# The output stores of an attention and FFN kernel, issued from ScalarE's queue in place of SyncE's

## The chip, the cores and the metric

The kernel runs on one core of one Trainium2 chip. The metric is the device time of one execution in microseconds. Three executions of the kernel before took 586.12, 587.52 and 589.68 us; the median is 587.52.

The engines are named as the profile names them: PE is the matrix engine (PEld its weight loads), DVE the vector engine, ACT the scalar engine, POOL GpSimd, and SP the sync engine, which does no arithmetic here and issues DMAs. A name with a q (SPq, ACTq) is the queue of that engine, where DMAs are issued and semaphores waited for.

## The reference

The function is a "talking heads" attention followed by a feed-forward network with a squared ReLU. Batch is 8, heads 12, sequence 448, head dimension 64, model dimension 768, hidden dimension 2048.

```python
scores = scale * np.matmul(q, k.transpose(0, 1, 3, 2))
scores = np.einsum('bhij,hg->bgij', scores, w_pre)      # heads mixed before the softmax
scores = scores - np.max(scores, axis=-1, keepdims=True)
attn = np.exp(scores)
attn = attn / (np.sum(attn, axis=-1, keepdims=True) + 1e-09)
attn = np.einsum('bhij,hg->bgij', attn, w_post)         # and after it
x = np.matmul(attn, v)                                  # transposed to (3584, 768)
h = np.maximum(x @ w_in, 0.0)
out = h * h @ w_out                                     # (3584, 768), float32
```

## The kernel before, in words

One program holds everything. The attention of a batch is cut into 45 steps of 10 query rows (`NT` = 45, `IQ` = 10). With 12 heads a step has 120 rows, one for each pair of query and head, so that the mixing of heads is a matmul over 120 partitions. There are 360 steps in all. The main loop over `i` makes, in each step, these pieces:

- `mix` (L415): one matmul (L426) mixes the heads of the gathered scores `G` into a PSUM bank `m_ps`; ACT takes the exponential with its row sum (L430) into `e`. Every second step DVE makes the reciprocals (L437) and POOL scales the second mixing matrix with them, `pn` (L440).
- `unmix` (L446), `LAG` = 4 steps later: matmuls of `e` with `pn` (L455, L459) into `at_ps`, which DVE copies (L461).
- `gather` (L382), up to `AHEAD` = 10 steps ahead: DMAs from SP's queue (L394, L397) that bring the scores of 10 queries of all heads from the score tile `S` into a `G` tile. `S` has two buffers, and `G` twelve.
- `score_burst` (L353): the matmuls of queries and keys (L365, L371) for six heads at once, each into a PSUM bank of its own; ACT (L375) and DVE (L377) copy them to `S`, about half each. A batch after the first takes seven bursts.
- `av_unit` (L221): after each third of a batch, the product with the values, copied by ACT to `xt` (L242).

Between these, `fill` lets out pieces of the feed-forward network of the batch before, which wait in a list with a cost each. `ffn1_unit` is the first matrix (L283), ReLU on ACT (L289) and a square on POOL (L295). `ffn2_unit` (L322) is the second matrix: 16 matmuls of 384 columns (L328) in two parts into one PSUM bank `o_ps`, and then a copy by DVE to half of an `osb` tile of 128 rows (L337). After the second half of a tile, `store_rows` (L305) stores its 128 rows. It issues one DMA for each stretch of up to `PQ` = 64 rows, because the rows of the output are interleaved over the sequence; so a tile of 128 rows needs two DMAs of 192 KB each, or one DMA for either of two batches where the tile holds the last 64 rows of both. That makes 54 DMAs in 27 pairs. `osb` has two buffers. The very last tile is stored in another way, by `last_store` (L313), half from SP's queue and half from ACT's.

All PSUM banks come from one pool of eight (`psp`, L77). The order of the instructions on PE and POOL is the order of the program text (`manual_schedule(engines={PE, POOL})`, L483). The order on ACT, DVE and SP, and with it the place of each store in its queue, is set by the framework's scheduler when the program is built. Each DMA from SP or ACT signals its landing on one of eight semaphores in turn, and before a DMA is issued its queue waits for the landing of the one that used the same semaphore before it.

Of the kernel before, what the change touches and what calls it, by code (L numbers as in the profile page):

```python
# [55 lines left out]
def kernel(  # L56
# [11 lines left out]
    nc = tc.nc  # L68
# [33 lines left out]
    def wcol(w, name, eng):  # L102
# [7 lines left out]
                      in_=bass.AP(tensor=w_pre.tensor, offset=w_pre[0, 0:1].offset, ap=[[0, P], [1, H * H]]))  # L110
# [24 lines left out]
    for t in range(3 * P // IQ, NT):  # L135
        n0, n = max(0, 3 * P - IQ * t), min(IQ, S - IQ * t)
# [166 lines left out]
    out_rows = out.rearrange("(b p r) m -> b r p m", b=B, r=RQ)  # L303

    def store_rows(b, t, end, osb, j):  # L305
        while t < end:
            r, p = divmod(t, PQ)
            n = min(end - t, PQ - p)
            nc.sync.dma_start(out=out_rows[b, r, p:p + n, :], in_=osb[j:j + n, :])
            t += n  # L310
            j += n

# [9 lines left out]
    def ffn2_unit(b, mt, nt, part):  # L322
        if part == 0:
            o_open[(b, mt, nt)] = bank("o_ps")
        ps = o_open[(b, mt, nt)]
        for ft in range(8 * part, 8 * part + 8):
            lhsT = h2ts[(b, ft // 2)][:, ft % 2, mt * P:mt * P + P] if mt < 3 else tails[:, ft, :]
            nc.tensor.matmul(ps[:, 0:384], lhsT=lhsT, rhs=w2[ft // 4][:, ft % 4, nt * 384:(nt + 1) * 384],  # L328
                             start=(ft == 0), stop=(ft == FT - 1))
        if part == 0:  # L330
            return
        if nt == 0:
            osbs[b] = ffnp.tile([P, DMODEL], F32, name="osb", tag="osb", bufs=2)
        if b == B - 1 and mt == 3:
            last_store(b, nt, osbs[b], ps)
            return
        nc.vector.tensor_copy(out=osbs[b][:, 384 * nt:384 * nt + 384], in_=ps[:, 0:384])  # L337
        if nt == 1 and mt < 3:
            store_rows(b, P * mt, P * mt + P, osbs[b], 0)
        elif nt == 1:  # L340
            store_rows(b - 1, MAIN, S, osbs[b], 0)
            store_rows(b, MAIN, S, osbs[b], 64)
# [140 lines left out]
    with tc.manual_schedule(engines={PE, POOL}):  # L483
# [40 lines left out]
        for i in range(-1, end):  # L524
# [9 lines left out]
            if s0:  # L534
                b, t = s0
# [75 lines left out]
```

## Time and profile before

| | before |
|---|---|
| median of three executions | 587.52 us |
| profiled execution, its own time | 588.54 us |
| its span, first to last instruction | 586.8 us |
| granted PE clock, mean | 0.996 |
| busy: PE, DVE, ACT, POOL | 563.8, 399.0, 379.6, 353.7 us |
| `store_rows`, issues on SP's queue | 54, of 466 to 1548 ns each, median 744 |
| first and last of them | 114.0 and 578.2 us |
| `gather`, issues of L394 on SP's queue | 312, of 672 to 2103 ns each, median 774 |
| DMAs issued on ACT's queue | 6: two at the start, four in `last_store` |

The busy times are those of one profiled execution. They overlap, so they don't add up to the span. Issuing a DMA or waiting for a semaphore doesn't count as busy time of ACT or SP: such time is found in the timeline of their queues. In lines of groups and waits, "out<-in" are tile names with buffer numbers left out. A line of waits gives who waited, for whom, the total in us, how often, and the longest; a line of the timeline gives the start in us, the length in us, the engine, the line and the operation, and in square brackets the idle time just before it and what ended that. The chain of work that ended last is followed back from the last instruction, and its rows give a start, a length and what ran.

### The profile page before, as it was taken

How to read it: one execution, taken by the hardware profiler on the slowest of the kernel's cores; microseconds unless marked ns; L12 is line 12 of the kernel's file. 1: busy time of each engine (PE TensorE's matmuls, PEld its weight loads, DVE VectorE, ACT ScalarE, POOL GpSimd, SP SyncE). 2: the span in 40 equal slices, each digit the busy share in tenths (PEclk: the TensorE clock that was granted, in tenths of full speed). 3: DMA queues.
4: the chain of work that ended last, by engine and by line, in shares of the span. 5: the costliest groups of instructions: out<-in, count | busy, mean ns of one | idle time of the engine just before them, and what ended most of it. 6: DMA issues, size and time to landing. Idle time of an engine off the chain costs nothing.

```text
span 586.8 us, 18426 instructions
## 1 busy us (share of the span) xinstructions
PE 563.8 (96%) x6735; PEld 363.8 (62%) x6735; DVE 399.0 (68%) x979; ACT 379.6 (65%) x1090; POOL 353.7 (60%) x796
## 2 busy tenths in 40 slices
PE   4999978999999999999999999999999999999996
PEld 2577767756566566566665665666565666666554
DVE  7748947868777677866977678767877668655011
ACT  3747967678876557875776558775777548862410
POOL 6566983574777338773678437783487436772730
PEclk9999998999999999999999999999999999999999
DMA  9999998596578864796559954788544865432113
GB/s 130 150 194 176 190 202 174 106 186 154 119 127 142 158 123 88 125 153 145 103 101 139 169 110 97 119 140 158 107 72 71 138 131 107 82 50 55 28 27 82
DMA packets 85579, 72.28 MB, mean 123 GB/s; under 512 B 18768, under 2 KB 80496, under 8 KB 85488
## 3 DMA queue, kind: packets, MB, share of 16 engines
q1 hardware_dynamic: 49354, 47.30, 36.5%
q0 software_dynamic: 35552, 23.60, 30.9%
q8 instruction: 53, 0.87, 0.6%
q10 hardware_dynamic: 582, 0.21, 0.2%
q14 instruction: 38, 0.31, 0.1%
HBM read 47.28 MB, written 11.01 MB: 99 GB/s over the span
## 4 chain that ended last, share of the span: by engine, by line
PE 91%; DMA 3%; ACT 3%; POOL 1%; DVE 1%; issue 1%; ACTq 0%; POOLq 0%
PE o_ps L328 25%; PE h_ps L283 25%; PE m_ps L426 11%; PE at_ps L455 10%; PE ot_ps L229 5%; PE s_ps L365 5%; PE m_ps L412 4%; DMA G<-S 2%; PE tr_ps L214 2%; PE ot_ps L236 2%; PE at_ps L459 2%; ACT e L430 1%; PE s_ps L371 1%; ACT S L375 1%; DMA kst<-in_k_dram 1%
## 5 line engine op out<-in xcount | busy, mean ns | idle before, releaser
L430 ACT ACTIVATE e<-m_ps 120x448 bf16<-120x448 f32 x360 | 196.1, 551 | 86.8 <-PE m_ps L426 46.7
L461 DVE CAST at<-at_ps 128x480 bf16<-128x480 f32 (+1 forms) x360 | 206.6, 593 | 65.9 <-PE at_ps L459 49.0
L440 POOL TENSOR_SCALAR pn<-post,rc 120x120 bf16<-120x120 bf16 (+1 forms) x340 | 123.4, 373 | 170.8 <-DVE rc L437 106.1
L283 PE MATMUL h_ps<-xt,w 128*128 128x448 bf16 (+2 forms) x960 | 167.2, 317 | 0.2
L328 PE MATMUL o_ps<-w,h 128*128 128x384 bf16 x768 | 138.7, 326 | 0.1
L426 PE MATMUL m_ps<-G,pre 120*120 120x448 bf16 (+1 forms) x340 | 121.8, 359 | 4.6 <-ACT S L375 3.1
L455 PE MATMUL at_ps<-pn,e 120*128 120x120 bf16 x1080 | 116.0, 216 | 4.3 <-ACT S L375 2.8
L283 PEld LDWEIGHTS <-w 128*128 128x128 bf16 x960 | 84.6, 99 | 53.4 <-issue 4.3
L455 PEld LDWEIGHTS <-e 120*128 120x128 bf16 x1080 | 86.0, 98 | 49.5 <-ACT S L375 5.4
L295 POOL TENSOR_TENSOR h<-hr 128x384 bf16<-128x384 f32 (+1 forms) x128 | 103.2, 807 | 20.4 <-ACT hr L289 19.1
L328 PEld LDWEIGHTS <-h 128*128 128x128 bf16 x768 | 72.9, 98 | 47.9 <-issue 4.9
L289 ACT ACTIVATE hr<-h_ps 128x448 f32<-128x448 f32 (+2 forms) x136 | 71.8, 530 | 45.4 <-PE h_ps L283 36.0
L375 ACT CAST S<-s_ps 128x448 bf16<-128x448 f32 x177 | 82.2, 550 | 15.3 <-PE s_ps L365 9.5
L377 DVE CAST S<-s_ps 128x448 bf16<-128x448 f32 x141 | 79.9, 615 | 5.1 <-DMA G<-S 4.3
L430 ACT ACTIVATION_READ_ACCUMULATOR e<-m_ps 120x1 f32 x360 | 75.5, 210 | 0.0
L337 DVE COPY osb<-o_ps 128x384 f32<-128x384 f32 x54 | 30.1, 557 | 57.6 <-PE o_ps L328 57.4
L437 DVE RECIPROCAL rc<-sm 120x1 f32<-120x1 f32 (+1 forms) x192 | 31.2, 163 | 43.0 <-ACT e L430 30.1
L426 PEld LDWEIGHTS <-pre 120*120 120x120 bf16 (+1 forms) x340 | 45.0, 132 | 22.1 <-issue 12.1
L242 ACT CAST xt<-ot_ps 128x450 bf16<-128x450 f32 (+1 forms) x48 | 25.7, 534 | 26.3 <-PE ot_ps L236 25.7
L443 POOL TENSOR_TENSOR en<-e,rc 120x128 bf16<-120x128 bf16 (+1 forms) x112 | 42.6, 380 | 0.0
L229 PE MATMUL ot_ps<-at,v 128*64 128x150 bf16 x864 | 41.6, 229 | 0.0
L459 PE MATMUL at_ps<-post,en 120*128 120x120 bf16 x181 | 39.1, 216 | 0.0
(62 smaller groups left out, 469.4 us busy)
## 6 DMA issues: line engine op xcount, KB each, us to landing
G<-S SPq DMA_DIRECT2D x276, 105.0 KB
out_dram<-osb SPq DMA_DIRECT2D x54, 192.0 KB
kst<-in_k_dram POOLq DMA_DIRECT2D x14, 336.0 KB, 7.1
qst<-in_q_dram POOLq DMA_DIRECT2D x14, 336.0 KB, 6.8
G<-S SPq DMA_DIRECT2D x70, 52.5 KB
v<-in_v_dram POOLq DMA_DIRECT2D x8, 384.0 KB, 8.6
w<-in_moe_w_in_dram POOLq DMA_DIRECT2D x6, 512.0 KB, 10.7
w<-in_moe_w_out_dram POOLq DMA_DIRECT2D x8, 384.0 KB, 8.8
```

The costliest lines, as they stand in the source:

```text
L229: nc.tensor.matmul(ps[64 * hh:64 * hh + 64, TQ * y:TQ * y + TQ], lhsT=vts[b % 2][:, g, r, :], rhs=at[:, r, g, :, :].rearrange("p t i -> p ...
L283: nc.tensor.matmul(ps[:, n * j:n * j + n], lhsT=w1[f // 8][:, c2, f % 8 * 128:f % 8 * 128 + 128], rhs=xts[b][:, c2, n0:n1], start=(c2 == 0 ...
L289: nc.scalar.activation(out=hr[:, 0:k * n], in_=ps[:, 0:k * n], func=ACT.Relu)
L295: eng.tensor_tensor(out=dst[:, :, x - o:y - o], in0=hr[:, :, x - n0:y - n0], in1=hr[:, :, x - n0:y - n0], op=ALU.mult)
L328: nc.tensor.matmul(ps[:, 0:384], lhsT=lhsT, rhs=w2[ft // 4][:, ft % 4, nt * 384:(nt + 1) * 384], start=(ft == 0), stop=(ft == FT - 1))
L375: nc.scalar.copy(out=sb[:, h, :], in_=ps[:, 0:S])
L377: nc.vector.tensor_copy(out=sb[:, h, :], in_=ps[:, 0:S])
L426: nc.tensor.matmul(ps[0:n, 0:S], lhsT=m[0:n, 0:n], rhs=Gs.pop(s)[0:n, :], start=True, stop=True)
L430: nc.scalar.activation(out=e[0:n, x, :], in_=ps[0:n, 0:S], func=ACT.Exp, scale=SCALE, accum_out=sm[0:n, x:x + 1])
L440: nc.gpsimd.tensor_scalar(out=esb[(b, t - z)][1][0:rows, :], in0=(post_gi if fused else post)[0:rows, :], scalar1=rc[0:rows, z:z + 1], sca ...
L455: nc.tensor.matmul(ps[:, RG * r:RG * r + RG], lhsT=e[0:n, tl % 2, P * r:P * r + P], rhs=pn[0:n, :], start=True, stop=True)
L461: nc.vector.tensor_copy(out=ats[(b, third)][:, 0:k, :, tl, :], in_=ps[:, 0:k * RG].rearrange("p (r g i) -> p r g i", r=k, i=IQ))
```

## The change

The DMAs that `store_rows` issues are issued by ACT (`nc.scalar`) in place of SP (`nc.sync`). Nothing else in the program text differs: the same rows are stored from the same tiles by the same number of DMAs, and `last_store` is left as it is. The scheduler orders ACT, DVE and SP anew for the changed program.

```diff
@@ -306,7 +306,7 @@ def store_rows(b, t, end, osb, j):
         while t < end:
             r, p = divmod(t, PQ)
             n = min(end - t, PQ - p)
-            nc.sync.dma_start(out=out_rows[b, r, p:p + n, :], in_=osb[j:j + n, :])
+            nc.scalar.dma_start(out=out_rows[b, r, p:p + n, :], in_=osb[j:j + n, :])
             t += n
             j += n
```

## The prediction

> **What bounds the kernel now.** I read the page's busy shares and chain first, then TensorE's waits, the stages in which stores are issued, and the queues of SP and ACT around single stores.
>
> From the page:
>
> ```profile
> PE 563.8 (96%) x6735; PEld 363.8 (62%) x6735; DVE 399.0 (68%) x979; ACT 379.6 (65%) x1090; POOL 353.7 (60%) x796
> PE 91%; DMA 3%; ACT 3%; POOL 1%; DVE 1%; issue 1%; ACTq 0%; POOLq 0%
> ```
>
> TensorE is the bound: 96% busy and 91% of the chain that ended last. ACT has about 207 us without work. So a change to ACT or SP counts only where it moves one of PE's waits. The waits of PE from 114 us (the first store) to 545 us:
>
> ```profile
> PE m_ps L426 <- ACT S L375: 3.1, 7, 1.7
> PE at_ps L455 <- DVE at L461: 0.9, 1, 0.9
> PE m_ps L426 <- ACT e L430: 0.3, 2, 0.2
> ```
>
> All of PE's waits there are 4.3 us; that is the most that the change can win. Two of the three name ACT, the engine that gets new work, and the largest is PE waiting for a PSUM bank that ACT empties after a burst of scores (L375).
>
> Busy time by stage, two with FFN2 and stores, one without:
>
> ```profile
> 188.00:216.00 28.00, 27.76 (x379) 18.65 (x376) 18.42 (x44) 14.23 (x42) 10.71 (x28) 1.00 0.78 145
> 320.00:352.00 32.00, 31.76 (x421) 21.27 (x418) 21.55 (x51) 16.77 (x51) 11.82 (x31) 1.00 0.78 143
> 352.00:395.00 43.00, 42.82 (x500) 26.47 (x497) 33.10 (x83) 33.84 (x98) 34.06 (x74) 1.00 0.70 120
> ```
>
> The fourth number of busy time is ACT's: about 51% where stores fall (14.23 of 28), 79% between them. The stores thus meet ACT in its emptier stages, with PE over 99% busy in both.
>
> **The price of an issue.** The SP queue around four stores, loaded stage and quiet tail:
>
> ```profile
> 206.69 1.72 SPq L309 DMA_DIRECT2D out_dram<-osb  x2
> 213.78 2.24 SPq L309 DMA_DIRECT2D out_dram<-osb  x2
> 484.78 2.01 SPq L309 DMA_DIRECT2D out_dram<-osb  x2
> 542.02 1.11 SPq L309 DMA_DIRECT2D out_dram<-osb  x2
> ```
>
> One `store_rows` call issues two DMAs of 192 KB and holds the queue 1.1 us when nothing else is issued, 1.5 to 2.4 us among gathers. The line's single issues go from 466 to 1548 ns, median 744. ACT issued stores beside SP once before, in the last tile (L320, two at 580.48 took 1.24 us, of 48 KB each). For a pair on ACT I bound the price by 1.06 us (the quiet single issues, 0.47 + 0.59) and 2.2 us, and take 1.7, the middle of the loaded pairs, because SP will still be issuing gathers beside it. That ACT does no other work meanwhile is seen at the start: the issue of L154 ends at 3.01 us and the table load of ACT starts at 3.04.
>
> **What is removed.** 54 issues in 27 groups leave SP, some 45 us of its queue; the gathers behind them (L394, L397) go out up to 1.7 us sooner after each. That matters where a gather ends a wait of PE. After the first store there is one such place on the chain:
>
> ```profile
> 130.92 1.46 DMA G<-S
> 132.40 0.54 ACT S L375
> ```
>
> Batch 1's burst waits for a score buffer until gathers have read it, ACT's copy follows, and PE stands 1.69 us (the longest in the first wait row). SP had spent 1.57 us on the store at 113.95 a little before. Worth 0 to 1.6 us; I take 0.8, since gathers wait for PE too. Elsewhere SP's own waits from 186 to 490 us are led by PE (34.3 us for m_ps L426), so SP isn't what holds gathers: 0.
>
> **What is added.** Each group puts on ACT a wait for the copy L337 and the pair. Queued behind are the next exponential (L430), a burst's copies (L375) or xt (L242); for them wait `unmix`, PSUM banks of a pool of eight, and FFN1. Where the store lands in ACT's order is up to the scheduler. The copy of 340.61 to 341.17 shows the usual place:
>
> ```profile
> 340.85 0.54 ACT L430 ACTIVATE e<-m_ps 120x448 bf16<-120x448 f32 x1 [1.01 <-POOL pn L440]
> 341.38 0.54 ACT L430 ACTIVATE e<-m_ps 120x448 bf16<-120x448 f32 x1
> 343.18 0.54 ACT L430 ACTIVATE e<-m_ps 120x448 bf16<-120x448 f32 x1 [1.17 <-POOL pn L440]
> ```
>
> An exponential becomes ready while the copy still runs, so I put the store behind it: the copy is done then, and the wait itself costs nothing. The exponential behind is late, but `unmix` uses it four steps later, about 6 us, so the lateness alone does no harm. It does where a burst comes before ACT has caught up: a burst takes six banks at once and in seven places PE waits for ACT there already. So for each of the 21 groups before 510 us I took ACT's idle time from the end of the copy to the first L375 after it, and compared it with what the pair took on SP. Twelve have more room than that (for example 5.45 us after 341.17) and cost nothing. Seven lack room, named by the copy's end: 142.10 (1.18 for 1.94, 0.76 short), 198.22 (0.62), 213.13 (1.43 for 2.24, 0.81), 277.91 (0.92), 348.13 (0.52), 412.93 (0.08), 484.13 (0.57 for 2.01, 1.44): together 5.15. Two, 262.01 and 397.10, fall into a running burst; I give them 0.5 each. Sum 6.2 us of lateness at bursts. Half reaches PE, because part of an issue runs while ACT still works on the exponential ahead (counted along ACT's timeline, 293 of its 432 semaphore instructions start under a running one) and not every bank is wanted at once: **3.1 us**, bounds 0.5 (pairs at 1.06, only 484.13 and the two in bursts still late) and 6.2.
>
> Smaller terms. The first group (copy ends 113.90) meets back-to-back exponentials at 75% ACT load: 0 to 1.6 us, I take 0.5. At 542.00 the last batch's xt is copied by ACT right after:
>
> ```profile
> 542.36 0.53 ACT L242 CAST xt<-ot_ps 128x444 bf16<-128x444 f32 x1 [7.76 <-PE ot_ps L236]
> 543.06 1.61 PE L283 MATMUL h_ps<-xt,w 128*128 128x448 bf16 x7
> ```
>
> A pair from 542.04 to 543.10 holds xt back 0.74 us, and PE starts FFN1 0.17 after xt: 0.6 (0 to 0.75). The three groups after 567 us meet an ACT that idles 17.97 us up to 580.13; the last issue ends before that: 0, as long as it does. `last_store` is unchanged. A wait for an earlier DMA's landing can move with the stores: SP's gathers had 12.5 us of it in 15 waits over all its issues, which shared by count is 1.4 us for 54 stores, on an engine with slack: 0.
>
> **Sum.** 3.1 + 0.5 + 0.6 - 0.8 = +3.4 us. On the profiled execution (588.54 us, 586.8 of it span) that is 591.9; it lies 1.0 over the median, so from the median of 587.52: **590.9**. The bounds together: from 0.5 - 1.6 = -1.1 (586.4) to 6.2 + 1.6 + 0.75 = +8.5 (596.0).
>
> **Rivals.**
>
> *The store stands ahead of the ready exponential* (slower). Then ACT's wait for the copy blocks it and nothing of the issue is hidden; that exponential, 0.551 + 0.210 us with its accumulator row, slides behind the pair. In 21 groups that is 0.76 us each, 16 in all; with half reaching PE as above +8 on the sum: 598.9. For it: the scheduler may see the copy end earlier than the chip does. Against: in the row above the exponential starts 0.32 us before the copy ends. It decides where the copy is ordered 0.3 us earlier.
>
> *SP's relief pays* (faster, the other side). Gathers leave sooner in the whole middle, the bursts start sooner, and most of PE's 4.3 us go while ACT's gaps take the stores: -3.3, 584.2. For it: the chain's gather of 1.46 us. Against: that is the only one after the first store, and the rest of the 4.3 us hangs on ACT and DVE. [...]
>
> *ACT isn't held by an issue, or its gaps take all* (no change): only the relief remains, -0.8, 586.7. For it: 51% load and gaps of about 1.1 us. Against: the table load at 3.04. [...]
>
> **How the numbers follow.** A measurement here can tell about 0.5% from no change, 2.9 us. Forecast 0.52 (own range 586.4 to 596; 0.32 of it above 590.4, 0.20 below), store ahead of the exponential 0.22, relief 0.10, nothing held 0.16. Slower 0.32 + 0.22 = 0.54, same 0.20 + 0.16 = 0.36, faster 0.10. A range of 585 to 599 leaves out about half of the relief case and half of the ahead case, 0.16.
>
> **What would show it.** Right: ACT's queue shows 54 more issues of 0.5 to 1.1 us each; PE's wait for ACT S (L375) and ACT e (L430) grows from 3.4 to about 6 us from 114 us on, in bursts after 142, 198, 213, 278 and 484 us; xt at 542 starts some 0.7 us later than the end of its matmuls; the 1.69 us at 131 shrink. Wrong: issues on ACT at 0.5 us throughout with PE's waits unchanged (gaps took all); issues that start before an exponential that was ready (ahead case); PE's waits below 2 us (relief).

## The result, and the profile after

The changed kernel takes 595.37 us in the median of six executions (592.56 to 596.55), against 589.51 for six of the kernel before (586.12 to 589.70). The ratio is 1.0098 with a 95% interval of [1.0075, 1.0121]: slower by 5.9 us. The forecast was slower by 3.4 us, to 590.9, with a range of 585 to 599.

The profiled execution took 592.56 us with a span of 590.6 us and a granted PE clock of 0.996. It is 4.0 us longer than the profiled execution before, and the shortest of the six. PE and POOL run the same order of instructions in both kernels; ACT, DVE and SP differ from the first store on (111.3 us in the changed kernel). So each matmul can be set against itself, and the difference of its two start times shows where the time went:

| place (start in the changed kernel) | after minus before, us |
|---|---|
| 94 to 112 us (no store can have had an effect) | -2.6 |
| 115 to 118 | -2.0 to -2.3 |
| 121.5 to 130.4 | -0.4 |
| last matmul ahead of PE's long wait there (after 130.99, before 130.94) | +0.05 |
| first matmul behind both waits, 134.0 | +1.0 |
| 138.7 | +2.8 |
| 151 to 201 | +3.8 |
| 213 to 419 | +4.0 to +4.5 |
| 431 to 544 | +3.1 to +3.5 |
| 557 to the end | +3.8 |

The lead at the top is not of the change's making: the kernel before had a granted clock of 0.89 in the mean from 85 to 100 us in its profiled execution, the changed kernel 1.00. (Of the twelve kernels below, eight have 0.89 there, two 0.77 and two 1.00.) What the change costs lies between 112 and 151 us, in the stage that stores batch 0; of it 4.2 us lie behind 130 us, around the second tile of that batch. The 20 pairs of later tiles that ACT issues between 190 and 540 us leave PE no later than it was, +3.8 ahead of them and +3.3 behind them.

The chain that ended last, by engine, shows who gained a share: PE had 91% before, ACT and DMA 3% each.

```profile
PE 87%; ACT 4%; DMA 4%; DVE 3%; issue 1%; ACTq 0%; POOL 0%; SPq 0%; DVEq 0%
```

The waits of PE after the first store, as before (who waited, for whom, total in us, times, longest):

```profile
PE s_ps L365 <- ACT e L430: 2.6, 2, 2.4
PE m_ps L426 <- ACT S L375: 2.4, 7, 0.9
PE h_ps L283 <- ACT xt L242: 0.6, 1, 0.6
PE m_ps L426 <- ACT e L430: 0.6, 4, 0.2
```

The first row is new: once, for 2.4 us, the first matmul of a score burst (L365) waited for a bank that an exponential had to empty. The forecast expected the waits for ACT's score copies (L375) and exponentials (L430) to grow from 3.4 to about 6 us, spread over later bursts. Their rows add up to 5.6, but nearly all of the growth is in that one wait: the seven waits behind the bursts' copies got shorter (3.1 to 2.4). The wait for xt is there with its 0.6. The place of the new wait in PE's timeline (start, length, line, in brackets the idle time before), the kernel before in the first block and the changed one in the second:

```profile
132.98 0.35 PE L426 MATMUL m_ps<-G,pre 120*120 120x448 bf16 x1 [1.69 <-ACT S L375]
```

```profile
130.99 0.35 PE L365 MATMUL s_ps<-kT,qT 64*128 64x448 bf16 x1 [0.26 <-DVE at L461]
133.75 0.35 PE L365 MATMUL s_ps<-kT,qT 64*128 64x448 bf16 x1 [2.41 <-ACT e L430]
```

And ACT's timeline there, before and after; ACTq rows are its queue:

```profile
129.50 0.55 ACT L430 ACTIVATE e<-m_ps 120x448 bf16<-120x448 f32 x1
...
132.40 1.84 ACT L375 CAST S<-s_ps 128x448 bf16<-128x448 f32 x4 [2.26 <-DMA G<-S]
```

```profile
128.07 0.54 ACT L430 ACTIVATE e<-m_ps 120x448 bf16<-120x448 f32 x1 [1.08 <-PE m_ps L426]
...
129.49 3.46 ACTq L309 DMA_DIRECT2D out_dram<-osb  x2
133.06 0.54 ACT L430 ACTIVATE e<-m_ps 120x448 bf16<-120x448 f32 x1 [4.36 <-DMA out_dram<-osb]
...
133.59 0.54 ACT L430 ACTIVATE e<-m_ps 120x448 bf16<-120x448 f32 x1
```

The two stores of one tile keep ACT from an exponential for 4.36 us, two are ready by then, and PE wants their banks. But the two issues themselves are short. The row takes 3.46 us because the second one starts only at 132.49, some 2.5 us after the first has ended.

What they waited for is seen where the trace gives each DMA's semaphore and landing. 53 of the 54 stores on ACT stand behind a wait for the semaphore that they signal themselves, and so for the landing of the DMA that used it before. For five of the six stores of batch 0's first three tiles that is a gather which SP issued and which lands just ahead of the store:

| store issued on ACT | that gather was issued | and landed |
|---|---|---|
| 111.30 | 105.56 | 111.11 |
| 112.67 | 108.59 | 112.65 |
| 129.49 | 125.68 | 129.42 |
| 132.49 | 127.38 | 132.46 |
| 145.56 | 139.55 | 145.48 |

Each of these starts 0.02 to 0.19 us after the landing. (The first of them also comes just behind its tile's copy, which ends at 111.27, so its start doesn't tell the two waits apart.) In the kernel before, the pair of the second tile stood further back in SP's queue: the copy ended at 128.60 and the issues came at 133.28 and 134.04, each 7.5 us behind the gather on its semaphore, which had landed 1.6 us or more before. ACT came to the first of them 1.3 us after its copy (128.22), 3.8 us behind the gather. So the move also brought the stores closer to the gathers whose landings they wait for.

From batch 1 on, the DMA that used the semaphore before (a gather or an earlier store) has landed 0.8 us or more before the store comes, and the issue costs PE nothing but the 0.6 us for xt:

```profile
201.82 0.54 ACT L430 ACTIVATE e<-m_ps 120x448 bf16<-120x448 f32 x1 [0.69 <-PE m_ps L426]
202.06 0.47 ACTq L309 DMA_DIRECT2D out_dram<-osb  x1
...
202.57 0.61 ACTq L309 DMA_DIRECT2D out_dram<-osb  x1
203.58 0.54 ACT L430 ACTIVATE e<-m_ps 120x448 bf16<-120x448 f32 x1 [1.13 <-POOL pn L440]
```

The first issue starts under a running exponential, and the next exponential waits for POOL as it did before. The DMA on this store's semaphore before was an earlier store (issued at 191.68), and it had landed at 195.44.

Part of the loss comes behind the wait. The stretch from 135 to 140 us, before and after (busy us and instructions of PE, PEld, DVE, ACT, POOL, then the granted PE clock, the DMA share, GB/s):

```profile
135.00:140.00 5.00, 4.96 (x43) 2.84 (x42) 4.26 (x11) 4.68 (x16) 2.22 (x7) 1.00 0.83 200
```

```profile
135.00:140.00 5.00, 5.00 (x33) 2.58 (x31) 3.42 (x8) 4.07 (x13) 2.78 (x7) 0.66 0.71 124
```

PE is busy throughout in both, but does 33 instructions in place of 43. Read us by us, the clock is 0.79 from 135, 0.50 from 136 to 139, and 1.00 again after it: half speed for 3.4 us, a loss of 1.7 us. The table of starts shows the same, +1.0 to +2.8 over these matmuls.

### The profile page after: what moved, and what is told of

It is laid out like the page before. It is cut to its first block, busy times and chain, and to the rows that moved or that the text cites. A ratio compares the mean times of both kernels' runs of the same rounds, so it can differ in the third digit from the quotient of the medians.

```text
span 590.6 us, 18418 instructions
## 1 busy us (share of the span) xinstructions
PE 564.8 (96%) x6735; PEld 363.3 (62%) x6735; DVE 398.2 (67%) x979; ACT 377.7 (64%) x1090; POOL 352.8 (60%) x796
## 4 chain that ended last, share of the span: by engine, by line
PE 87%; ACT 4%; DMA 4%; DVE 3%; issue 1%; ACTq 0%; POOL 0%; SPq 0%; DVEq 0%
PE o_ps L328 24%; PE h_ps L283 24%; PE m_ps L426 11%; PE at_ps L455 9%; PE ot_ps L229 4%; PE s_ps L365 4%; PE m_ps L412 4%; DMA G<-S 3%; PE tr_ps L214 2%; ACT e L430 2%; PE at_ps L459 2%; PE ot_ps L236 1%; ACT S L375 1%; PE s_ps L371 1%; DVE w L197 1%
## 5 line engine op out<-in xcount | busy, mean ns | idle before, releaser
L430 ACT ACTIVATE e<-m_ps 120x448 bf16<-120x448 f32 x360 | 196.3, 552 | 92.2 <-PE m_ps L426 58.6
L461 DVE CAST at<-at_ps 128x480 bf16<-128x480 f32 (+1 forms) x360 | 206.5, 592 | 65.5 <-PE at_ps L459 48.3
L426 PE MATMUL m_ps<-G,pre 120*120 120x448 bf16 (+1 forms) x340 | 121.5, 358 | 3.3 <-ACT S L375 2.4
L283 PEld LDWEIGHTS <-w 128*128 128x128 bf16 x960 | 83.4, 98 | 54.1 <-issue 4.7
L375 ACT CAST S<-s_ps 128x448 bf16<-128x448 f32 x177 | 82.6, 553 | 16.6 <-PE s_ps L365 9.2
L430 ACT ACTIVATION_READ_ACCUMULATOR e<-m_ps 120x1 f32 x360 | 76.1, 211 | 0.0
L365 PE MATMUL s_ps<-kT,qT 64*128 64x448 bf16 x276 | 39.1, 359 | 3.4 <-ACT e L430 2.6
```

The costliest lines, as they stand in the source:

```text
L283: nc.tensor.matmul(ps[:, n * j:n * j + n], lhsT=w1[f // 8][:, c2, f % 8 * 128:f % 8 * 128 + 128], rhs=xts[b][:, c2, n0:n1], start=(c2 == 0 ...
L375: nc.scalar.copy(out=sb[:, h, :], in_=ps[:, 0:S])
L426: nc.tensor.matmul(ps[0:n, 0:S], lhsT=m[0:n, 0:n], rhs=Gs.pop(s)[0:n, :], start=True, stop=True)
L430: nc.scalar.activation(out=e[0:n, x, :], in_=ps[0:n, 0:S], func=ACT.Exp, scale=SCALE, accum_out=sm[0:n, x:x + 1])
L461: nc.vector.tensor_copy(out=ats[(b, third)][:, 0:k, :, tl, :], in_=ps[:, 0:k * RG].rearrange("p (r g i) -> p r g i", r=k, i=IQ))
```

## The experiments

Two theories stood at first. The landing theory (theory A below): the cost is the wait of batch 0's stores for earlier landings, in front of a burst. The room theory (theory B) is that of the prediction: issues make ACT late in bursts all along. Each edit and each ratio is against the kernel before, on the same chip; `...` stands for code left out of an edit.

**Stores of batch 0 back on SP, all others on ACT.**

```diff
-            nc.sync.dma_start(...
+            (nc.scalar if b > 0 else nc.sync).dma_start(...
```

> Stores of batch 0 (three tiles at 111, 129 and 145 us in the profile of the changed kernel, and its share of the tile at about 213 us) go back to SP's queue; the other batches stay on ACT's. Theory A: the cost sits in batch 0's stores, where ACT waits for landings of earlier DMAs and the DMA engines are over 80% busy; the later stores cost only the late xt near 543 us. It expects 0 to +1.5 us against the kernel before, so that 4 us or more of the change's loss come back. Theory B, the main term of the prediction: lateness at the bursts of batches 1 to 7; it expects +3 to +5 us against before.

Measured: 589.94 us, 1.0005 [0.9985, 1.0026]. With 47 of 54 issues on ACT the whole loss is gone. PE's waits keep xt and no row of L365:

```profile
PE m_ps L426 <- ACT S L375: 3.6, 7, 2.1
PE at_ps L455 <- DVE at L461: 1.0, 1, 1.0
PE h_ps L283 <- ACT xt L242: 0.6, 1, 0.6
```

The room theory falls for batches 1 to 7. One of these stores did wait for a landing: the second of the pair at 189 us, whose gather was issued at 184.13 and landed at 189.89.

```profile
189.91 0.58 ACTq L309 DMA_DIRECT2D out_dram<-osb  x1
190.53 0.97 ACT L242 CAST xt<-ot_ps 128x450 bf16<-128x450 f32 x2 [1.33 <-PE at_ps L459]
```

ACT is idle for 1.33 us there, and PE's waits from 180 to 200 us are 0.5 us in all. So this wait of 1.33 us cost nothing measurable: PE didn't yet want what stood behind it.

**Only the stores of batch 0 on ACT.**

```diff
+            (nc.scalar if b == 0 else nc.sync).dma_start(...
```

> The converse: only batch 0's stores are issued from ACT's queue, all others from SP's as before. Theory A expects +4 to +6 us against before, the whole loss but the 0.6 of xt. Theory B expects 0 to +1.5 us.

Measured: 594.44 us, 1.0097 [1.0064, 1.0131]. The seven DMAs of batch 0 carry the whole loss. The new wait of PE is there, and longer:

```profile
PE s_ps L365 <- ACT e L430: 4.8, 2, 4.7
```

**Only one tile, the second of batch 0, on ACT.**

```diff
+            (nc.scalar if b == 0 and P <= t < 2 * P else nc.sync).dma_start(...
```

> Only the second tile of batch 0 (stored at about 129 us) is issued from ACT's queue: one pair of DMAs in the whole kernel. Theory A with the landing wait as its mechanism: the second DMA of the pair stands 2 us or more in ACT's queue for the landing of the DMA that used its semaphore before, PE's wait at 131 us is longer by 1 us or more than before, +1.5 to +4 us in all. If it is only the time of the issue itself (about 1 us): 0 to +1 us. Theory B: 0.

Measured: 595.22 us, 1.0104 [1.0071, 1.0138]. One pair of DMAs, two of 54, costs as much as all of them by the medians. That is 5.9 us, more than the 1.5 to 4 that the landing theory expected, which had no slow clock behind the wait. ACT's timeline at that pair:

```profile
130.38 0.54 ACT L430 ACTIVATE e<-m_ps 120x448 bf16<-120x448 f32 x1 [1.08 <-PE m_ps L426]
...
134.66 3.16 ACTq L309 DMA_DIRECT2D out_dram<-osb  x2
137.93 0.54 ACT L430 ACTIVATE e<-m_ps 120x448 bf16<-120x448 f32 x1 [6.92 <-DMA out_dram<-osb]
```

The gathers of these two semaphores were issued at 128.50 and 130.51 and landed at 134.59 and 137.28, each just ahead of its store. PE's wait of this kind is 5.0 us here. Its matmuls stand +1.9 us against the kernel before ahead of that place, +6.1 behind the wait and +8.3 at 153 us, with the clock at half speed from 137.3 to 144.1.

**Batch 0 and the tile ahead of the last xt back on SP.**

```diff
+            (nc.scalar if b > 0 and not (b == 6 and 2 * P <= t < MAIN) else nc.sync).dma_start(...
```

> As the first of these, and the third tile of batch 6 (stored at 542 us just ahead of the last batch's xt) also goes back to SP. The prediction's xt term: PE's wait of 0.6 us for xt at about 543 us is gone, 0.6 us less than the first of these; against before -0.8 to +1 by theory A. Theory B: +2.5 to +4.5 us.

Measured: 589.13 us, 1.0000 [0.9977, 1.0024]. The wait for xt is gone from PE's list and the step in PE's starts at 543 us with it (+0.95 to +1.66 with only batch 0 on SP, none here). The medians differ by 0.8 us, which the intervals can't tell from nothing. It is the best of the versions with stores on ACT, and it doesn't beat the kernel before.

**Loads of the next batch moved later, with and without that one tile on ACT.** POOL issues loads of keys, queries and values between 114 and 132 us; the idea was to free the DMA engines while the gathers land.

```diff
-KQ_LATER = {1: (26, 28, 37, 41), B: (22, 25, 28, 31)}
-V_LATER = {1: (30, 32, 34), B: (34, 37, 40)}
+KQ_LATER = {1: (38, 40, 49, 53), B: (22, 25, 28, 31)}
+V_LATER = {1: (42, 44, 46), B: (34, 37, 40)}
```

> As the kernel with one tile of batch 0 on ACT's queue, and the seven loads of batch 2's values and batch 3's queries and keys, which GpSimd issues at 114 to 132 us, come 12 steps later (about 18 us). Theory A, landing wait: the gathers ahead of the store then land in about 4 us in place of 6, ACT stands 1 us or less for them, PE's wait at 131 us for ACT e (L430) is under 1.5 us, and the time is at most 1.5 us above that of the next kernel, which has the moved loads alone. Theory C, the pair costs by standing ahead of two exponentials whatever the landings do: 4 to 6 us above the next kernel.

> The kernel before with the same seven loads 12 steps later, all stores on SP's queue: the measure for the kernel just above. Both theories expect -2 to +1 us against before; below zero if PE's wait of 1.7 us at 131 us, which a gather's landing ends, gets shorter.

Measured: 592.55 us, 1.0055 [1.0033, 1.0078], with the tile on ACT; 592.24 us, 1.0037 [1.0010, 1.0063], without. Inconclusive: the loads went only to 126.7 to 149.3 us in the first and 123.7 to 144.4 us in the second, onto the store itself. The second is slower than the kernel before by 2.7 us, where -2 to +1 was expected. The gathers of 126 to 136 us still took 5.9 and 7.3 us in the median, ACT still stood, and PE waited 3.2 us in the first; in the second PE waits 2.3 us for a gather at the same burst, so that the pair on ACT adds nothing measurable here.

**ACT held by other work, stores on SP.** Two copies of 128x384 on ACT, written behind each pair's second copy (four in the second kernel, `4 * nt`), stand for the time of the issues, without any DMA.

```diff
+        ...; [nc.scalar.copy(out=scr[:, :], in_=osbs[b][:, 384 * (y % 2):384 * (y % 2) + 384]) for y in range(2 * nt)]
```

> The kernel before, stores on SP's queue, but after each pair's second copy ACT makes two extra copies of 128x384 from the tile (into a scratch tile that nothing reads), some 1 us of ACT's time in 27 places: the time of a pair of issues without its wait for a landing. Theory A: 0 to +1.5 us, no wait of PE over 2 us at 131 us. If the time on ACT were the cost: +4 to +6 us, like the changed kernel.

> The same with four extra copies, some 2 us of ACT in 27 places, above the price at which the prediction counted 6.2 us of lateness at bursts and half of it lost. If that count of room is right and only the price was off: +3 to +7 us, with PE's waits for ACT in bursts after 142, 198, 213, 278 and 484 us. If ACT's slack is larger than the count: up to +2 us.

Measured: 588.62 us, 0.9987 [0.9965, 1.0010], and 589.87 us, 1.0004 [0.9983, 1.0025]. The group of the second kernel (busy us and mean ns, then idle before):

```profile
L337 ACT CAST scr<-osb 128x384 bf16<-128x384 f32 x108 | 55.4, 513 | 17.5 <-DVE osb L337 16.2
```

55.4 us more work on ACT, about 2 us for each tile, cost nothing. This speaks against the time of the issues as the price, with a reservation: the copies do not stand where the edit puts them. Some of them read the tile's first half only, and the scheduler puts one for each tile some 4 us ahead of the second copy; others stand between exponentials. Until 530 us they hold ACT at most 0.56 us in one piece in the first kernel and 1.6 us (three copies) in the second, never 3.5 us.

**The loads moved out of the stage.** The same as above with `KQ_LATER[1] = (26, 28, 54, 57)` and `V_LATER[1] = (59, 61, 63)`, with the one tile on ACT and without.

> The kernel with one tile of batch 0 on ACT's queue again, and now only batch 2's values and batch 3's queries are loaded later, 24 to 29 steps, so that none of these five loads falls between 118 and 140 us; the two loads of keys stay at 114 to 118 us. (12 steps had moved them right onto the store.) Theory A, landing wait: gathers issued at 126 to 136 us land in about 4 us, not 6; ACT's queue stands for them 1.5 us or less; the time is at most 1.5 us above the next kernel. Theory C, the pair costs by its place in ACT's order alone: 4 to 6 us above the next kernel.

> The kernel before with the same five loads later, all stores on SP's queue: the measure for the kernel just above. Both theories: -2 to +1 us against before; if PE's 1.7 us at 131 us, which a gather's landing ends, go away, about -1.5.

Measured: 599.17 us, 1.0163 [1.0139, 1.0187], with the tile; 596.24 us, 1.0105 [1.0089, 1.0121], without. The late loads cost 6.5 us by themselves, where -2 to +1 was expected (PE waits 5.5 us for values at 164 to 166 us in the second). The difference is 2.9 us, between what the theories expected. The gathers of 126 to 136 us now land in 4.4 us, but the two that matter were issued only at 124.81 and 126.52, shortly ahead of the store, and landed at 127.44 and 131.30, so ACT still stood:

```profile
127.51 4.33 ACTq L309 DMA_DIRECT2D out_dram<-osb  x2
131.94 0.54 ACT L430 ACTIVATE e<-m_ps 120x448 bf16<-120x448 f32 x1 [4.69 <-DMA out_dram<-osb]
```

PE's wait was 2.7 us. Landings of 4.4 us alone did not remove the wait here: it also counted how long ahead of the store the gather was issued. So the pair costs half as much here, and the cause isn't isolated.

**A landing waited for on ACT, without a store on it.** All stores on SP. SP also issues one transfer of 72 KB within SBUF at the second tile of batch 0, and ACT makes a small copy of what it brings.

```diff
+        ...; (b == 0 and mt == 1 and nt == 1) and (nc.sync.dma_start(out=scr[0][:, :], in_=osbs[b][:, 384:528]),
+                                                   nc.scalar.copy(out=scr[1][:, :], in_=scr[0][:, :]))
```

> No store on ACT's queue at all. At the second tile of batch 0 (about 129 us) SP issues one added transfer of 72 KB from the tile into a scratch tile, and ACT makes one small copy of it (0.3 us), which stands in its order inside the burst that follows: ACT only waits for a landing, and issues nothing. Theory A (the wait for a landing is the cost): the transfer lands some 6 us after its issue at 133 us, PE waits for ACT in this burst 4 us or more longer than before, +4 to +9 us. If issuing from ACT is the cost: within 1 us of before.

Measured: 596.42 us, 1.0119 [1.0095, 1.0143], with not one store issued by ACT. Its timeline:

```profile
132.50 0.53 ACT L375 CAST S<-s_ps 128x448 bf16<-128x448 f32 x1 [2.23 <-DMA G<-S]
139.34 0.31 ACT L337 COPY scr<-scr 128x144 f32<-128x144 f32 x1 [6.31 <-DMA scr<-osb]
139.56 1.39 ACT L375 CAST S<-s_ps 128x448 bf16<-128x448 f32 x3
```

PE waited 6.4 us for ACT's score copies:

```profile
PE at_ps L455 <- ACT S L375: 6.4, 1, 6.4
```

SP issued the transfer at 133.66, and ACT stood until it had landed at 139.32. A landing waited for on ACT in this place is enough to lose all that the change loses. ACT stood longer here (6.31 us) than in the change (4.36), and inside the burst's copies in place of ahead of the exponentials, so the size isn't to be compared.

**The same at the second tile of batch 1** (`b == 1`).

> The same at the second tile of batch 1 (about 198 us), where gathers land in about 4 us and the burst begins 2 us after the copy: theory A: ACT stands there some 3 us, +1.5 to +4 us, less than the kernel just above. If issuing from ACT is the cost: within 1 us of before.

Measured: 588.14 us, 0.9978 [0.9961, 0.9995]: no loss. The expectation is missed. ACT waited there too, but not as long:

```profile
202.77 0.31 ACT L337 COPY scr<-scr 128x144 f32<-128x144 f32 x1 [1.38 <-DMA scr<-osb]
```

SP issued the transfer at 199.42; ACT had work until 201.38 and stood 1.38 us, and PE waited 0.2 us in the whole burst. The place decides: in batch 0 the same transfer took 5.7 us, here 3.3, and in batch 0 ACT had nothing left to do. Why this kernel comes out 0.2% under the one before is not explained.

## Why the prediction was right in sign and range, and wrong in place

**Where it failed: "on an engine with slack: 0".** The prediction knew of the wait for an earlier DMA's landing. It had it as 12.5 us in 15 waits over all of SP's issues, shared it by count to 1.4 us for 54 stores, and set it to nothing. In the change one such pair holds ACT 3.46 us, and by the kernel with that pair alone it carries the whole loss. The average hid that these waits aren't spread: in the kernel before, the gathers of 112 to 136 us took 6.0 to 6.2 us to land in the median, those of 150 to 520 us 3.9. It also missed that ACT comes to a store earlier than SP did, 3.8 us behind its gather in place of 7.5. "An engine with slack" was wrong likewise, because the slack has to be there in the right place. By the prediction's own count of room the pair behind the copy of 128.60 costs nothing: ACT is idle for 2.26 us there ahead of the first score copy (the row at 132.40), and the pair took 1.73 us on SP. With the wait for the landing it took 3.46. That is 1.2 us over the room, just ahead of a burst that wants six of eight banks, and PE's wait is longer by about as much (1.0 us). The trace shows where the wait was spent: ACT stood 4.36 us without work, and either issue began less than 0.1 us behind the landing on its semaphore (129.49 after 129.42, 132.49 after 132.46). The change moved not only the issue but that wait onto the engine that empties the banks.

**Missing altogether: the clock.** In the profiled execution PE's wait, net of the one that the kernel before has there, is about 1.0 us; the half clock behind it adds 1.7 (+1.0 to +2.8). No term of the sum had that.

**The largest term, 3.1 us at bursts, measured about 0.** Its inputs were too high: the median issue on ACT took 496 ns, after 744 on SP, and the median pair 1.09 us in place of the 1.7 taken (five of 27 took 2.1 to 2.2), and part of it runs under an exponential. And its rule, that half of ACT's lateness at a burst reaches PE, has nothing to stand on: with batch 0 back on SP all these issues cost nothing, and the extra copies, 1 and 2 us more on ACT for each tile, moved nothing either.

**First group, 0.5:** the medians don't show it: with all three tiles of batch 0 on ACT the time is 594.44 us, with the second tile alone 595.22. PE's starts do: right behind this pair they fall back 0.4 us in the change (-2.6 to -2.2) and in the kernel with only batch 0 on ACT (+1.7 to +2.1), where PE waits 0.38 us for DVE's copy L461, and not in the kernel with the second tile alone (+1.9 throughout). So the size is near; that the path goes over ACT isn't shown. In the profiled execution of the change a further 1.8 us go there (-2.2 to -0.4), not by ACT's issues: a gather beside the two stores took 6.65 us to land, at 118.33, and the burst's copies waited for it. **Late xt, 0.6:** 0.6 in PE's waits and in the starts, right. **SP's relief, -0.8:** it isn't seen: PE's wait at 131 gave way to a longer one for ACT.

**The rivals.** The store ahead of the ready exponential has the mechanism nearest to what happened: exponentials that are ready stand behind a store that waits. But what it waits for is a landing, not the copy, and it happens in one stage, not in 21 groups. The relief of SP fell: PE's own waits did not go. That ACT isn't held by an issue did not show, and the reading of the table load at 3.04 stands for new exponentials and copies: an exponential that has begun goes on under an issue (the store at 202.06), but in none of the 54 does a new exponential or copy start before the issue has ended; the next one starts 0.04 us or more behind it. The other half of this rival came true from batch 1 on: the gaps take the issues. Its total was wrong because of the wait.

So the measured time fell into the range by luck, for another reason than the one given: a term of 3.1 us that measured about 0, in place of one that was set to nothing and measured 5.9 us (one tile on ACT alone).

**What stays open.** The two profiled executions differ by 4.0 us, the medians by 5.9. The profiled execution of the change is the shortest of its kernel, has no half clock at 85 to 100 us and waits 2.4 us at the burst; with the same second tile on ACT the two reduced kernels have that half clock, wait 4.7 and 5.0 us, and take 596.86 and 595.67 us in their profiled executions. So 5 us may be the usual wait. The granted clock speaks for it: 0.989 to 0.990 in the other five executions of the change, as in the profiled ones of the two reduced kernels (0.990 and 0.989), against 0.996 in the profiled one of the change. But only that one was profiled. Whether the 1.8 us at 118 us come from the stores' transfers or from the early start is open too. Between 145 and 151 us, behind the third tile's pair on ACT, PE falls back by another 1.3 us (+2.5 to +3.8), of which 0.5 is in small waits of PE; it falls back 0.7 us there with only batch 0 on ACT and not at all with the second tile alone. The medians don't show that either. A store on ACT whose semaphore no gather uses, and a hold of ACT of 3.5 us in one piece without a landing, were not tried.

## What to carry to other kernels

Here the move of the stores to a compute engine's queue moved what they wait for as well, and the issue time was the smaller part of the price: of the 3.46 us of the longest pair the two issues took 0.95, the rest went to the landing of the DMA that last used the second one's semaphore, and ACT's ready exponentials queued behind it (4.36 us without work). Look for the one stage where landings are slow (6.0 to 6.2 us here, 3.9 later), the DMA comes soon behind the one on its semaphore (3.8 us, 7.5 from SP), and the engine is wanted next, not at the average over all issues. A sum that comes out right is no proof of its terms: undo the change for one stage at a time and see which of them carries it.

## What the runs showed of the hardware that was not expected

- Behind a wait of PE of 2.41 us the granted clock fell to 0.50 for 3.4 us, while PE was busy again (135.6 to 139.0 us). Behind waits of 4.7 and 5.0 us (only batch 0, and only its second tile, on ACT) it was 0.50 for 6.8 us, twice as long; but it was so around a wait of 2.7 us as well (loads moved out, one tile on ACT), and behind 3.2 us (loads moved later, one tile on ACT) it was 3.4. In the same place 1.69 us (the kernel before) and 2.1 us (batch 0 on SP) left it at 1.00, and 2.2 us (the kernel with the added transfer at batch 1, whose wait at 131 us is not of that transfer's making) took it to 0.50 for 3.4 us. So the length of the wait alone doesn't settle it. But for the last, the profile's stretches of one clock are multiples of 3.41 us (75.09, 3.41 and 491.52 before; 119.47, 3.41 and 450.56 in the change). What sets that step, and what brings half clock, no run here shows.
- An issue on ACT runs beside an exponential that has started (the issue from 202.06 to 202.53, the exponential from 201.82 to 202.36). The read of its accumulator starts under the issue too (0.19 us from 202.26), as at 17 of the 54 issues. No exponential or copy that stands behind one of the 54 starts under it; the next one comes 0.04 us or more after its end.
- In the kernel before, the same kind of gather took 6.0 to 6.2 us to land in the median at 112 to 136 us and 3.9 at 150 to 520 us. The profile's DMA share was 0.94 to 1.26 in the stretches of 5 us from 115 to 135 us and 0.47 to 0.78 in the stages from 150 to 510 us.
